# Seven block products in place of eight: key, query and feed-forward projections as Strassen units ahead of attention

## The chip, the cores and the metric

The kernel runs on one core of one Trainium2 chip. A core has five engines that run their own instruction streams and meet through semaphores: TensorE (PE; it multiplies matrices, and loads the stationary operand, called the weights, in a stream of its own, PEld), VectorE (DVE), ScalarE (ACT), GpSimd (POOL) and SyncE (SP, which here only starts transfers). PE writes its results into PSUM, eight banks of 128 x 512 floats; all other operands lie in SBUF. The metric is the time of one launch in microseconds (us).

## The reference

`x` is 2048 x 640. Two paths share it: a 32-head attention in four segments of 512 rows with a compressive memory, and a gated feed-forward block. A sigmoid gate mixes them.

```python
q, k, v = x @ wq, x @ wk, x @ wv            # 32 heads of 20
for s in range(4):                          # segments of 512 rows
    p = softmax(q[s] @ k[s].T * 20**-0.5 + mask)
    a_dot = p @ v[s]
    a_mem = phi(q[s]) @ M / (phi(q[s]) @ z + 1e-6)
    o[s] = g * a_mem + (1 - g) * a_dot
    M += phi(k[s]).T @ v[s];  z += phi(k[s]).sum()
a = o @ wo
b = (silu(x @ w1) * (x @ w3)) @ w2          # 640 -> 1728 -> 640
out = gate * a + (1 - gate) * b
```

Here `phi(t)` is `t + 1` for positive `t` and `exp(t)` otherwise. The results are wanted in float32 quality.

## The kernel before, in words

**Precision.** Each float32 matrix is split into a rounded high part and the rest (`split`, L115; `parts`, L290; `w_split`, L178). A product is three passes (`PASSES`, L261): high x high, high x low, low x high. With the contraction of 640 in five blocks of 128 (kb), one output block of 128 features x 512 rows is 15 matmuls of 512 columns (`proj`, L263).

**Chunks.** The 2048 rows are four chunks of 512 (c = 0 to 3), handled as two pairs, A = (0, 1) and B = (2, 3).

**Head.** Ahead of attention the program computes, for A: query blocks 0 and 1 (`q_blocks`), all values (`v_blocks`, L378), the five key blocks of each chunk (`k_block`, L423) and query block 2. Between the key blocks stand the memory steps: a transpose of phi(k) (`memory_turn`, L441: pkt) and its product with v (`memory_write`, L453: pm).

**Attention with filler.** Then 32 quads of four heads follow (`attention`, L810). Each quad has 40 slots. In a few slots stands a visit, a bundle of scores for the row maxima (s, L647), scores in transposed form (t, L682) and products with v (o, L703); `VISITS` (L807) says which bundle stands in which slot. A quad's s, t and o stand in three successive quads: the row maxima go from DVE (L654) by ACT, DVE and a transfer into two extra rows of `qk`, and only then t can run. Between the visits PE gets "dense" filler in portions: the rest of the projections, the feed-forward blocks (gate g and up u, `ffn_up`, L520; down f, `ffn_down`, L579) and the output projection (op). The jobs are listed in segments (`segs`), and each segment's work is spread evenly over the slots up to its end.

**Order and buffers.** PE's order is as the program is written. The other engines' order is set by a scheduler at build time, so they are in-order queues in a fixed order when they run. Weights go through six W buffers in rotation (NW, L27); POOL makes the two parts of each from W7 on (the cast L185, the subtraction L190). PSUM banks are given out in rotation (`bank_tile`, L121); a bank in which dense products accumulate is held until they are done.

Of the kernel before, what the change touches and what calls it, by code (L numbers as in the profile page):

```python
# [30 lines left out]
EARLY = range(2, 6)  # L31
OUT = {5: (0, 1), 6: (2, 3)}
# [6 lines left out]
def gated_mix(ctx: ExitStack, tc: tile.TileContext, xT, w01, wqk, wv, w13, w2, w2h, wo, beta, out):  # L39
# [81 lines left out]
    def bank_tile(name, hold=None):  # L121


        k = free.pop(0)
# [8 lines left out]
    def filled():  # L133

        free.extend(held)
        held.clear()
# [20 lines left out]
    items, tiles = [], {}  # L157

    def w_add(src, n, queue=nc.sync):
        items.append((src, n, queue))  # L160
        return len(items) - 1

    early, raws, clock = [], [], dict(step=0, oldest=2, next=2)

    def w_load():
        k = clock["next"]
        src, n, queue = items[k]
        if k in EARLY:
            if k % 2 == 0:
                early[:] = [sp.tile([P, 2, 1280], F32, tag="P32", name=f"wr{k}", bufs=NP)]  # L170
            raw = early[0][:, k % 2]
        else:
            raw = sp.tile([P, D + 2], F32, tag="wraw", name=f"wr{k}", bufs=NRAW)
        queue.dma_start(raw[:, :n], src)
        raws.append([k, raw, n, clock["step"]])
        clock["next"] += 1

    def w_split():  # L178
        k, raw, n, _ = raws.pop(0)
        w = sp.tile([P, 2, D + 2], FR, tag="W", name=f"W{k}", bufs=NW)  # L180
        tiles[k] = w
        if k < 7:
            split(w[:, :, :n], raw[:, :n], lo=nc.vector.tensor_sub)
        else:
            hi = nc.gpsimd.tensor_copy(w[:, 0, :n], raw[:, :n])  # L185
# [4 lines left out]
            last["low"] = nc.gpsimd.tensor_sub(w[:, 1, :n], raw[:, :n], w[:, 0, :n].bitcast(F32))  # L190

    def w_step():
# [3 lines left out]
        if raws and raws[0][0] in EARLY:  # L196
            if clock["step"] >= 6 + 2 * raws[0][0]:
                w_split()
        elif raws and raws[0][0] < clock["oldest"] + NW and \
                clock["step"] - raws[0][3] >= (AGE if "exp" in last or raws[0][0] < 7 else 2 * AGE + 1):  # L200
            w_split()
        if sum(r[0] not in EARLY for r in raws) < NRAW and clock["next"] < min(len(items), clock["oldest"] + NW + NRAW):
            w_load()

    def w_get(i, oldest=None):

        while i not in tiles:
            if not raws or raws[-1][0] < i and len(raws) < NRAW:
                w_load()
            else:  # L210
                w_split()
        clock["oldest"] = i if oldest is None else oldest
        return tiles[i]

# [225 lines left out]

    def memory_turn(c, mb):  # L441
# [76 lines left out]
    hts = {}  # L518

# [59 lines left out]
    def ffn_down(cs, js, idx, last=()):  # L579
        first = js[0] == 0  # L580
        w2s = [w_get(i, idx[0]) for i in idx]
        for c in cs:
# [135 lines left out]
    def o_sums(c):  # L718
# [4 lines left out]
        after(22 if c < NSEG - 1 else 3, o_scale, c, er)  # L723
# [85 lines left out]

    def attention():  # L810

        for m in range(-1, NQUAD + 2):
            for n in range(40):
# [3 lines left out]
                todo = VISITS.get(n, ()) if m != 1 else {BIG: VISITS[BIG][:3] + VISITS[BIG][4:5], BIG + 6: VISITS[BIG][5:]}.get(n, VISITS.get(n, ()))  # L817
# [10 lines left out]
                elif n in ((24, 36) if m < 0 else (BIG + (1 if m > 1 else 7), SMALL + 1)) and m + 1 < NQUAD:  # L828
# [43 lines left out]
    def job_up(cs, j):  # L872
        return (4 if j < NF else 2) * 3.5, ffn_up(cs, j, plan_up([j])[0])
# [72 lines left out]
    segs.append((2 * H - 2, seg))  # L946
# [23 lines left out]
    for n, (_, g) in enumerate(head):  # L970
# [3 lines left out]
        if n == 0:  # L974
            constants()
        elif n == 2:
            selection()
        elif n == 7:
            gates()
    stores(True)  # L980
    att = attention()
# [115 lines left out]
```

## Time and profile before

| what | value |
|---|---|
| runs of this kernel | 1099.22, 1099.38, 1100.0 us (median 1099.38) |
| profiled execution: its own time, from first to last instruction (span) | 1098.7 us |
| PE busy | 1093.1 us, 99% |
| PEld / DVE / ACT / POOL busy | 78% / 55% / 35% / 53% |
| HBM traffic over the span | 138 GB/s |

The page gives no other time for the profiled execution than its span; the median of the runs lies 0.7 us above it. The busy share is that of whole engines over all stages; matmuls are pipelined, so that the duration shown for one (some 0.4 us) is longer than the distance from one to the next. That distance is read from the chain of waits, where a run of matmuls stands with its count and its whole time.

### The profile page before, as it was taken

Reading aid. Unit: us, or ns where it says so; the run is one execution under the profiler, and the core shown is the slowest. Engines: PE = TensorE matmul, PEld = TensorE weight load, DVE = VectorE, ACT = ScalarE, POOL = GpSimd, SP = SyncE. Lnnn points to the kernel's source line nnn. Section 1 sums busy time; section 2 is a strip of 40 time slices with the busy share of each in tenths; the row PEclk is TensorE's granted clock in tenths of the full one; section 3 lists DMA queues with packets and bytes.
Section 4 is the critical chain, followed back from the end, with each engine's and each line's share of the span. In section 5 each row is a group of like instructions: output and inputs, shape, how many; then the busy total and the mean of one; then the engine's idle time right before and its main releaser. Section 6 shows DMA issues by size and latency. Waiting matters only on the chain.

```text
span 1098.7 us, 17910 instructions
## 1 busy us (share of the span) xinstructions
PE 1093.1 (99%) x6289; PEld 853.6 (78%) x6289; DVE 603.1 (55%) x1716; ACT 381.9 (35%) x829; POOL 584.2 (53%) x729
## 2 busy tenths in 40 slices
PE   9999999999999999999999999999999999999998
PEld 7988887777777777778977777777777777777787
DVE  6032474356555554566153678975657765551575
ACT  6244233443233122145244543424333332223020
POOL 5055556366366363566066447656674655565263
PEclk9999999999999999999999999999999999999999
DMA  9266943334355234435367966445664343432122
GB/s 314 105 207 222 284 123 82 95 83 117 77 141 124 58 85 124 137 83 184 112 201 264 298 216 185 112 148 140 161 149 111 96 113 97 111 102 89 52 79 96
DMA packets 87978, 153.21 MB, mean 139 GB/s; under 512 B 11632, under 2 KB 25872, under 8 KB 87888
## 3 DMA queue, kind: packets, MB, share of 16 engines
q1 hardware_dynamic: 63472, 106.30, 30.3%
q0 software_dynamic: 20384, 38.68, 15.6%
q10 hardware_dynamic: 4032, 7.08, 1.8%
q8 instruction: 50, 0.82, 0.3%
q14 instruction: 40, 0.33, 0.1%
HBM read 96.56 MB, written 54.54 MB: 138 GB/s over the span
## 4 chain that ended last, share of the span: by engine, by line
PE 99%; DMA 0%; ACT 0%; DVE 0%; SPq 0%; issue 0%
PE g L267 18%; PE f L593 18%; PE u L267 17%; PE o L703 7%; PE v L398 7%; PE op L852 6%; PE k L267 6%; PE q L267 5%; PE s L647 5%; PE t L682 4%; PE nd L365 2%; PE pm L462 1%; PE q L338 1%; PE gt L783 1%; PE pkt L447 1%; PE rr L777 0%
## 5 line engine op out<-in xcount | busy, mean ns | idle before, releaser
L654 DVE CUSTOM_DVE_ANT_0 junk<-s,mask 128x256 bf16<-128x256 f32 (+3 forms) x512 | 250.4, 489 | 106.1 <-PE s L647 74.0
L688 ACT ACTIVATE P<-t 128x512 f32<-128x512 f32 (+1 forms) x384 | 172.5, 536 | 187.7 <-PE t L682 145.1
L267 PE MATMUL g<-X,W 128*128 128x512 f32 x840 | 208.9, 398 | 0.1
L190 POOL TENSOR_TENSOR W<-wr,W 128x640 fp32r<-128x640 f32 (+1 forms) x126 | 198.8, 1583 | 2.5
L267 PE MATMUL u<-X,W 128*128 128x512 f32 x780 | 196.9, 399 | 0.0
L593 PE MATMUL f<-ht,W 128*128 128x512 f32 (+1 forms) x825 | 196.4, 395 | 0.0
L185 POOL CAST W<-wr 128x640 fp32r<-128x640 f32 (+1 forms) x126 | 92.6, 739 | 195.1 <-PE v L398 44.6
L693 POOL TENSOR_SCALAR_AFFINE_SELECT P<-P 128x256 f32<-128x256 f32 x192 | 93.6, 497 | 179.5 <-ACT P L688 179.2
L267 PEld LDWEIGHTS g<-X,W 128*128 128x128 f32 x840 | 155.8, 188 | 37.3 <-DVE m L654 0.4
L593 PEld LDWEIGHTS f<-ht,W 128*128 128x128 f32 x825 | 153.1, 188 | 36.3
L267 PEld LDWEIGHTS u<-X,W 128*128 128x128 f32 x780 | 144.0, 188 | 34.5 <-ACT P L688 0.3
L117 POOL TENSOR_TENSOR ht<-ft,ht 128x512 fp32r<-128x512 f32 x52 | 67.5, 1298 | 91.1 <-ACT ht L116 91.0
L624 POOL DMA_DIRECT2D qk<-qkd x128 | 83.3, 652 | 0.5 <-issue 0.2
L647 PE MATMUL s<-qk 60*128 60x256 f32 (+3 forms) x512 | 77.7, 346 | 0.0
L267 PE MATMUL k<-X,W 128*128 128x512 f32 x300 | 77.2, 404 | 0.0
L703 PE MATMUL o<-P,vg 128*32 128x512 f32 (+3 forms) x1024 | 75.5, 435 | 0.1
L533 ACT ACTIVATE ft<-g 128x512 f32<-128x512 f32 x52 | 31.2, 600 | 126.5 <-PE g L267 113.8
L534 DVE SCALAR_TENSOR_TENSOR fu<-ft,g 128x512 f32<-128x512 f32 x52 | 35.6, 685 | 67.9 <-ACT ft L533 58.8
L398 PE MATMUL v<-W,X 128*128 128x320 f32 (+1 forms) x480 | 72.1, 311 | 0.2 <-ACT P L688 0.2
L398 PEld LDWEIGHTS v<-W,X 128*128 128x128 f32 x480 | 71.2, 189 | 0.9 <-ACT P L688 0.4
L116 ACT CAST ht<-ft 128x512 fp32r<-128x512 f32 x52 | 32.2, 619 | 109.9 <-DVE ft L542 108.1
L601 DVE TENSOR_TENSOR acc<-f,acc 128x512 f32<-128x512 f32 x65 | 44.8, 689 | 39.5 <-PE f L593 39.2
(125 smaller groups left out, 1209.3 us busy)
## 6 DMA issues: line engine op xcount, KB each, us to landing
qk<-qkd POOLq DMA_DIRECT2D x128, 240.0 KB, 4.1
wr<-in_w_dram SPq DMA_DIRECT2D x80, 320.0 KB
qkd<-qs SPq DMA_DIRECT2D x20, 512.0 KB
qkd<-ks SPq DMA_DIRECT2D x20, 512.0 KB
od<-oq SPq DMA_DIRECT2D x32, 256.0 KB
wr<-in_wo_dram SPq DMA_DIRECT2D x20, 320.0 KB
vg<-vd SPq DMA_DIRECT2D x16, 336.0 KB
xr<-in_xT_dram SPq DMA_DIRECT2D x20, 256.0 KB
```

Of the source, the lines that this page charges most:

```text
L117: (lo or nc.gpsimd.tensor_sub)(dst[:, 1], src, dst[:, 0].bitcast(F32))
L185: hi = nc.gpsimd.tensor_copy(w[:, 0, :n], raw[:, :n])
L190: last["low"] = nc.gpsimd.tensor_sub(w[:, 1, :n], raw[:, :n], w[:, 0, :n].bitcast(F32))
L267: nc.tensor.matmul(ps, w[:, a, kb * P:(kb + 1) * P], x[:, b, kb, :], start=n == 0, stop=n == 14)
L398: nc.tensor.matmul(ps[:, :n1 - n0], x[:, a, kb, lb * P:(lb + 1) * P], wvt[kb][:, b, n0:n1], start=n == 0, stop=n == 14)
L593: nc.tensor.matmul(ps[:, :n1 - n0], w, h, start=n == 0, stop=n == len(ms) - 1)
L624: here(nc.gpsimd.dma_start(t[64 * i:64 * i + RH], qkd[c][RH * (h + i):RH * (h + i + 1)]))
L647: nc.tensor.matmul(ps[i][:, o:o + w], q[:, qb * P:(qb + 1) * P], key[:, :w], start=n == 0, stop=n == len(todo) - 1, skip_group_check=True)
L654: r = nc.vector.tensor_tensor_reduce(out=junk[:, :w], in0=ps[i][:, o:o + w], in1=mask[:, L - w:], scale=1.0, scalar=-3.0e38, op0=ALU.add, ...
L688: last["exp"] = nc.scalar.activation(pairs[2 * m + k]["P"][:, i, o:o + n], ps[i][:, b:b + n], AF.Exp, scale=SCALE)
L693: nc.gpsimd.affine_select(d, d, pattern=[[0, 2], [0, n], [1, P]], base=0, channel_multiplier=-1, compare_op=ALU.is_ge, fill=0.0)
L703: nc.tensor.matmul(ps[32 * i:32 * i + 32, kb * P:], heads[2 * p + i]["v"][:, kb], pairs[p + i // 2]["P"][:, i % 2, o:o + n], start=kb == 0 ...
```

## The change

Four pairs of key and query blocks (K0 K1, K2 K3, K4 Q2, Q3 Q4) and the gate/up pairs of four feature blocks (0, 1, 2 and 3) are computed for chunks 0 and 1 as "units" (`unit`). A unit treats its two weight blocks, the two chunks and the first four contraction blocks as 2 x 2 matrices of blocks and forms seven products in place of eight, with sums and differences of the operands; the fifth contraction block is computed as before. The sums of the four x blocks are made once (`build_sums`, braided with the values), from x loaded again; they lie in `qk` and two wide buffers. For each unit DVE makes five sums of weight blocks (`w_split`, kind "sum0"), POOL splits four weight operands (of 640, 640, 512 and 384 columns), and the results are put together by DVE and ACT in the buffers W, V and G.

All eight units stand ahead of attention, with the down product of feature blocks 0 to 2 between the third and the fourth feed-forward unit. Thus query blocks 3 and 4 and a part of the feed-forward work leave attention's filler, and the job lists of the first two segments are shorter. Further edits: `ffn_down` of the first two groups starts with three feature blocks side by side (`lead`: three held banks) and with chunk 1 or 3 first; the visits of the first two quads are spread by a table of their own (`FIRST`); constant rows of `qk` and `vg` are set by DVE behind the units; the loads of the first two head pairs are issued in the last unit.

```diff
-        for v in vg:
-            nc.gpsimd.memset(v[:, :, VG:], 0.0)
-        one = cp.tile([P, KB, L], F32, tag="oall", name="one", bufs=1)[:, 0]
-        nc.gpsimd.memset(one, -1.0)
-        for i in range(4):
-            nc.gpsimd.tensor_copy(qk[i // 2][:, 1, i % 2], one)
+    def fixed_rows():
+        for t in qk:
+            nc.vector.memset(t[:, 1].bitcast(F32), -1.0)
+        nc.vector.memset(vg[0][:, :, VG:], 0.0)
...
+        elif kind == "sum0":
+            low = raws[rs[1]][0]
+            sums[rs[1]] = t = f_tile(f"ws{k}")
+            a11, a12, a15 = raw[:, :2 * P], raw[:, 2 * P:4 * P], raw[:, 4 * P:D]
+            a21, a22, a25 = low[:, :2 * P], low[:, 2 * P:4 * P], low[:, 4 * P:D]
+            nc.vector.tensor_add(t[:, 2 * P:], a21, a22)
+            nc.vector.tensor_sub(t[:, :2 * P], a11, a21)
+            nc.vector.tensor_sub(a11, t[:, 2 * P:], a11)
+            nc.vector.tensor_sub(a12, a12, a11)
+            nc.vector.tensor_sub(a15, a15, a25)
...
+    def build_sums(cs):
+        c0, c1 = cs
+        raw, two = {}, []
+        def load(i):
+            for n, (c, kb) in enumerate(((c1, 2 + i), (c1, i), (c0, i), (c0, 2 + i))):
+                raw[i, n] = f_tile(f"tr{c0}_{i}_{n}")
+                nc.sync.dma_start(raw[i, n], xT[c, :, kb, :])
...
+            b22, b12, b11, b21 = (raw[i, n] for n in range(4))
+            nc.vector.tensor_sub(b22, b22, b12)
+            nc.vector.tensor_sub(b12, b12, b11)
+            nc.vector.tensor_add(b11, b22, b11)
+            split(out(2, i), b11, lo=nc.vector.tensor_sub)
+            yield 1
+            split(out(1, i), b12, lo=nc.vector.tensor_sub)
+            nc.vector.tensor_sub(b21, b21, b11)
+            yield 1
+            split(out(3, i), b22, lo=nc.vector.tensor_sub)
+            yield 1
+            split(out(4, i), b21, lo=nc.vector.tensor_sub)
...
+    def unit(cs, name, idx, take, W, V, G):
+        c0, c1 = cs
+        T = lambda n: lambda i, b: Ts[n, i][:, b]
+        B = lambda c, kb: lambda i, b: Xs[c][:, b, kb + i]
+        def product(ps, w, col, x, n, start=False, stop=False):
+            t = 0
+            for i in range(n):
+                for a, b in PASSES:
+                    nc.tensor.matmul(ps, w[:, a, col + i * P:col + (i + 1) * P], x(i, b),
+                                     start=start and t == 0, stop=stop and t == 3 * n - 1, skip_group_check=True)
+                    t += 1
+                if i < n - 1:
+                    yield 699
+        w0, wa, wb, wl = idx
+        U = w_get(w0, w0)
+        a, ka = bank_tile(f"{name[0]}{c0}_{name}", 1300), last["k"]
+        yield from product(a, U, 0, B(c0, 0), 2, True, True)
+        nc.scalar.copy(W, a)
+        yield 699
+        S0 = w_get(wa, w0)
+        w, kw = bank_tile(f"w{c0}_{name}", 1300), last["k"]
+        yield from product(w, S0, 0, T(2), 2, True, True)
+        filled(kw)
+        nc.vector.tensor_add(W, W, w)
+        yield 699
+        S1 = w_get(wb, w0)
+        x, kx = bank_tile(f"x{c1}_{name}", 1300), last["k"]
+        yield from product(x, S1, 2 * P, T(1), 2, True)
+        yield 699
+        A2 = w_get(wl, w0)
+        yield from product(x, A2, 2 * P, B(c1, 4), 1, False, True)
+        nc.scalar.copy(V, x)
+        yield 699
+        y, ky = bank_tile(f"y{c0}_{name}", 1300), last["k"]
+        yield from product(y, S1, 0, T(3), 2, True, True)
+        nc.vector.tensor_add(V, V, y)
+        nc.vector.tensor_add(V, V, W)
+        gone.add(wb)
+        if name[0] != "f":
+            take(1, c1, V)
+        yield 699
+        yield from product(a, U, 2 * P, B(c0, 2), 2)
+        yield 699
+        yield from product(a, U, 4 * P, B(c0, 4), 1, False, True)
+        filled(ka)
+        gone.add(w0)
+        take(0, c0, a)
+        yield 699
+        yield from product(x, S0, 2 * P, B(c1, 2), 2)
+        yield 699
+        yield from product(x, S0, 4 * P, B(c1, 4), 1, False, True)
+        filled(kx)
+        gone.add(wa)
+        g = G if G is not None else f_tile(f"ug{name}")
+        nc.vector.tensor_add(g, W, x)
+        take(0, c1, g)
+        if name[0] == "f":
+            take(1, c1, V)
+        yield 699
+        yield from product(y, A2, 0, T(4), 2)
+        yield 699
+        yield from product(y, A2, 2 * P, B(c0, 4), 1, False, True)
+        filled(ky)
+        nc.vector.tensor_add(W, W, y)
+        take(1, c0, W)
+        clock["oldest"] = wl + 1
...
+        def take(i, c, ps):
+            w, mb = blocks[i]
+            if w:
+                big["k", c, mb] = phi = pks.pop(0)
+                out.append((c, mb))
+            else:
+                phi = big["q", c][:, mb * L:(mb + 1) * L] if c else None
+            store_parts(w, c, mb, parts(f"{'qk'[w]}s{c}_{mb}", ps, phi))
...
+            if i == 0:
+                us[c] = u = f_tile(f"fu{c}_{j}")
+                nc.scalar.activation(u, ps, AF.Tanh, scale=0.5)
+                nc.vector.scalar_tensor_tensor(u, u, 1.0, ps, op0=ALU.add, op1=ALU.mult)
+            else:
+                nc.vector.scalar_tensor_tensor(us[c], us[c], 0.5, ps, op0=ALU.mult, op1=ALU.mult)
+                split(hts[c, j], us[c], lo=nc.vector.tensor_sub)
+            if i == 0 and c == cs[0] and j == sum(GROUPS[:2], [])[2 + NU]:
+                fixed_rows()
+                for p in range(2):
+                    load_pair(p)
...
+        lead = js in GROUPS[:2]
+        for c in cs[::-1] if lead else cs:
             if first:
                 accs[c] = slot(f"acc{c}")[:, :KB * L].rearrange("p (b n) -> p b n", b=KB)
-            for fb in range(KB):
+            if lead:
+                two = [bank_tile(f"f{c}_{js[0]}_{fb}_0", 1300) for fb in range(3)]
+                for n, j in enumerate(js):
+                    for fb, ps in enumerate(two):
+                        for i, (a, b) in enumerate(PASSES):
+                            nc.tensor.matmul(ps, w2s[n][:, b, fb * P:(fb + 1) * P], hts[c, j][:, a],
+                                             start=n == i == 0, stop=(n, i) == (len(js) - 1, 2))
+                        yield 699
+                filled()
+                for fb, ps in enumerate(two):
+                    dst = accs[c][:, fb]
+                    if first:
+                        nc.scalar.copy(dst, ps)
+                    else:
+                        nc.vector.tensor_add(dst, ps, dst)
+            for fb in range(3 if lead else 0, KB):
...
+    s, t = (lambda f: ("s", 0, f)), (lambda f: ("t", 1, f))
+    FIRST = ({5: (s(0),), 8: (s(2),), 11: (s(1),), 14: (s(3),), 17: (s(4),)},
+             {5: (s(0), t(0), t(1), t(3)), 11: (s(2), t(2), s(1)), SMALL: VISITS[SMALL]})
...
-    head = qa + job_v(A)
+    head = qa + [braid(chain(job_v(A)), (0, build_sums(A)), 3)]
     load_wide(1)
-    ka, turns, writes = jobs_k(A)
-    q2 = job_q(A, 2)
-    head += ka + q2[:1] + turns + q2[1:] + writes
+    K0, K1, K2, K3, K4 = ((1, mb) for mb in range(KB))
+    head += jobs_qk(A, ((K0, K1), (K2, K3), (K4, (0, 2)), ((0, 3), (0, 4))))
+    head += [job_unit(A, j) for j in GROUPS[0]] + [job_down(A, 0)]
+    head += [job_unit(A, j) for j in GROUPS[1][:NU]]
+    clock["wide"] = len(items)
     segs = []
-    seg = job_q2(A, 3)
-    g = jobs_group(A, 0)
-    seg += [braid(chain(g[:2]), job_read(1), 3, at=(7, 10, 13, 16, 18, 22, 25, 28))] + g[2:] + jobs_group(A, 1) + jobs_up(A, 2)
+    seg = [job_up(A, j) for j in GROUPS[1][NU:]] + [job_down(A, 1)]
+    g = jobs_group(A, 2)
+    seg += [braid(chain(g[:2]), job_read(1), 3, at=(9, 12, 15, 18, 21, 24, 27, 30))] + g[2:] + jobs_up(A, 3)
     segs.append((H + LAG + 1, seg))
-    d = job_down(A, 2)
-    u = [job_up(A, j) for j in GROUPS[3][:2]]
+    d = job_down(A, 3)
     o1, o2 = jobs_oproj(0)
-    seg = [d, braid(chain(u), o1, 5), o2] + [job_up(A, j) for j in GROUPS[3][2:]] + [(0, load_shares(A[:1])), job_down(A, 3)]
+    seg = [braid(d, o1, 3, at=(13, 15, 17, 19, 20)), (0, load_shares(A[:1])), o2]
```

**PE, the start of the key stage.** In the names k is a key block, then the chunk (`k0_...`); ge is a small transpose; in the changed kernel w, x, y are further products of the unit, W7 to W10 the four weight operands, T and qk the sums of x, X0 and X1 the chunks. Before:

```order
L267 MATMUL k0_0_618<-X0_103,W7_276 128x512 x9
L419 MATMUL ge0_628<-ident_88,gate_102 8x128
L267 MATMUL k0_0_618<-X0_103,W7_276 128x512 x6
L267 MATMUL k1_0_647<-X1_105,W7_276 128x512 x9
L419 MATMUL ge1_670<-ident_88,gate_102 8x128
L267 MATMUL k1_0_647<-X1_105,W7_276 128x512 x6
L447 MATMUL pkt0_0_688<-ident_88,pk0_0_639 128x128 x4
L267 MATMUL k0_1_695<-X0_103,W8_594 128x512 x12
L462 MATMUL pm0_0_711<-V0_302,pkn0_0_693 128x147 x4
```

Now:

```order
L544 MATMUL k0_k0k1_664<-X0_103,W7_268 128x512 x6
L544 MATMUL w0_k0k1_685<-qk1_91,W8_626 128x512 x6
L469 MATMUL ge0_694<-ident_88,gate_102 8x128
L544 MATMUL x1_k0k1_698<-qk0_90,W9_643 128x512 x6
L469 MATMUL ge1_705<-ident_88,gate_102 8x128
L544 MATMUL x1_k0k1_698<-X1_105,W10_651 128x512 x3
L544 MATMUL y0_k0k1_714<-T0_319,W9_643 128x512 x3
L544 MATMUL y0_k0k1_714<-T1_447,W9_643 128x512 x3
L544 MATMUL k0_k0k1_664<-X0_103,W7_268 128x512 x9
L544 MATMUL x1_k0k1_698<-X1_105,W8_626 128x512 x9
L544 MATMUL y0_k0k1_714<-T0_319,W10_651 128x512 x3
```

Key blocks 0 and 1 of both chunks were 60 matmuls on two weight operands; they are now 54 matmuls on four. The second operand, W8, is now wanted after 6 matmuls; before it was wanted after 30.

**POOL, the same place.** `CAST` makes a weight operand's high part, `TENSOR_TENSOR` its low part. Before:

```order
L99 AFFINE_SELECT sel_96<-sel_96 32x640
L102 COPY sel_96<-sel_96 32x640 x2
L185 CAST W8_594<-wr8_271 128x640
L185 CAST W9_605<-wr9_279 128x640
L190 TENSOR_TENSOR W8_594<-wr8_271,W8_594 128x640
L190 TENSOR_TENSOR W9_605<-wr9_279,W9_605 128x640
L174 DMA wr10_597<-in_wqk_dram 128x640
L174 DMA wr11_608<-in_wqk_dram 128x640
```

Now:

```order
L186 DMA wr8_263<-in_wqk_dram 128x640
L226 TENSOR_TENSOR W7_268<-wr7_181,W7_268 128x640
L221 CAST W8_626<-wr7_181 128x640
L221 CAST W9_643<-ws8_627 128x512
L221 CAST W10_651<-wr8_263 128x384
L221 CAST W11_668<-wrs_292 128x640
L226 TENSOR_TENSOR W8_626<-wr7_181,W8_626 128x640
L226 TENSOR_TENSOR W9_643<-ws8_627,W9_643 128x512
L226 TENSOR_TENSOR W10_651<-wr8_263,W10_651 128x384
```

Four casts now stand ahead of the subtraction that completes W8; before there were two.

**PE in the middle of attention, quad 26.** s, t are scores of the quad in the name, f is a down product. Before, from the end of the first visit of the quad to its second:

```order
L647 MATMUL s26_1_0_9150<-qk0_90 128x384
L647 MATMUL s26_1_1_9151<-qk0_90 128x384
L647 MATMUL s26_1_0_9150<-qk0_90 128x128
L647 MATMUL s26_1_1_9151<-qk0_90 128x128
L593 MATMUL f3_3_1_0_9167<-ht3_3_8444,W97_8454 128x512 x3
L593 MATMUL f3_3_1_0_9167<-ht3_4_8587,W98_8530 128x512 x3
L593 MATMUL f3_3_1_0_9167<-ht3_5_8823,W99_8691 128x512 x3
L593 MATMUL f3_3_2_0_9178<-ht3_3_8444,W97_8454 128x512 x3
L593 MATMUL f3_3_2_0_9178<-ht3_4_8587,W98_8530 128x512 x3
L593 MATMUL f3_3_2_0_9178<-ht3_5_8823,W99_8691 128x512 x3
L593 MATMUL f3_3_3_0_9189<-ht3_3_8444,W97_8454 128x512 x3
L593 MATMUL f3_3_3_0_9189<-ht3_4_8587,W98_8530 128x512 x3
```

Now:

```order
L892 MATMUL s26_1_0_9294<-qk0_90 128x384
L892 MATMUL s26_1_1_9295<-qk0_90 128x384
L892 MATMUL s26_1_0_9294<-qk0_90 128x128
L892 MATMUL s26_1_1_9295<-qk0_90 128x128
L892 MATMUL s26_3_0_9311<-qk0_90 128x256
L892 MATMUL s26_3_1_9312<-qk0_90 128x256
L892 MATMUL s26_3_0_9311<-qk0_90 128x256
L892 MATMUL s26_3_1_9312<-qk0_90 128x256
L927 MATMUL t25_4_0_9325<-qk1_91 128x384
L927 MATMUL t25_4_1_9326<-qk1_91 128x384
L927 MATMUL t25_4_0_9325<-qk1_91 128x128
L927 MATMUL t25_4_1_9326<-qk1_91 128x128
```

The 24 dense matmuls that stood between the two visits are gone from there; the second visit now follows the first at once.

## Rows read from the trace of the kernel before

**Rows 1.** Page, first line and section 1: PE's busy time

```profile
span 1098.7 us, 17910 instructions
...
PE 1093.1 (99%) x6289; PEld 853.6 (78%) x6289; DVE 603.1 (55%) x1716; ACT 381.9 (35%) x829; POOL 584.2 (53%) x729
```

**Rows 2.** Page, section 2: granted TensorE clock in 40 slices (9: full speed)

```profile
PEclk9999999999999999999999999999999999999999
```

**Rows 3.** Waits of PE: engine, line <- whom: us in total, times, longest

```profile
PE warm L921 <- DVE zero L918: 1.3, 1, 1.3
PE q L338 <- ACT w01s L116: 0.2, 1, 0.2
PE v L398 <- ACT P L688: 0.2, 1, 0.2
```

**Rows 4.** Chain of waits in order of time: start us, us, what

```profile
22.32 33.89 PE v L398 x227
...
68.83 2.83 PE k L267 x12
73.80 2.79 PE k L267 x12
...
353.15 20.99 PE f L593 x90
```

**Rows 5.** Stretches of the values and the keys: us, busy time and instructions by engine

```profile
25.00:50.00 25.00, 25.00 (x171) 25.00 (x170) 0.52 (x3) 5.55 (x18) 3.66 (x6) 1.00 0.35 128
75.00:100.00 25.00, 25.00 (x137) 21.43 (x136) 7.62 (x15) 12.17 (x28) 16.54 (x26) 1.00 0.68 228
```

**Rows 6.** Timeline from 50 to 62 us: start us, us, engine, line, what

```profile
54.56 1.38 POOL L185 CAST W<-wr 128x640 fp32r<-128x640 f32 x2 [25.71 <-PE v L398]
55.91 3.09 POOL L190 TENSOR_TENSOR W<-wr,W 128x640 fp32r<-128x640 f32 x2
...
56.06 2.27 PE L267 MATMUL k<-X,W 128*128 128x512 f32 x9
...
57.53 1.49 DVE L413 TENSOR_SCALAR gate<-gate 128x4 f32<-128x4 f32 x1
```

**Rows 7.** Page, section 5: groups of instructions, busy us, mean ns

```profile
L654 DVE CUSTOM_DVE_ANT_0 junk<-s,mask 128x256 bf16<-128x256 f32 (+3 forms) x512 | 250.4, 489 | 106.1 <-PE s L647 74.0
...
L190 POOL TENSOR_TENSOR W<-wr,W 128x640 fp32r<-128x640 f32 (+1 forms) x126 | 198.8, 1583 | 2.5
...
L601 DVE TENSOR_TENSOR acc<-f,acc 128x512 f32<-128x512 f32 x65 | 44.8, 689 | 39.5 <-PE f L593 39.2
```

**Rows 8.** Groups by form: a DVE subtraction with both inputs in SBUF

```profile
L786 DVE TENSOR_TENSOR oall<-on,gm 128x512 fp32r<-128x512 f32 x15 | 13.6, 915 | 2.1 <-ACT gm L785 2.1
```

**Rows 9.** Tile X on DVE: ns min/median/max

```profile
L117 DVE TENSOR_TENSOR X<-xr,X x7: 692/694/3148, 4.2 to 13.7; 128x512 fp32r<-128x512 f32 x7
```

**Rows 10.** Timeline from 385 to 392 us: one POOL and one DVE subtraction

```profile
387.69 1.29 POOL L117 TENSOR_TENSOR ht<-ft,ht 128x512 fp32r<-128x512 f32 x1 [0.88 <-ACT ht L116]
388.23 1.30 DVE L786 TENSOR_TENSOR oall<-on,oT 128x512 fp32r<-128x512 f32 x1 [0.69 <-ACT oT L785]
```

**Rows 11.** Chain of waits in order of time, 760 to 781 us

```profile
760.97 0.43 PE s L647 x2
...
765.48 3.67 PE f L593 x15
769.14 0.43 PE s L647 x4
...
770.10 2.98 PE f L593 x12
...
780.09 0.43 PE s L647 x2
```

More of the change, by code (lines that the diff above doesn't have):

```diff
@@ L131, in bank_tile, with filled @@
         return ps
[L133 to L136 removed]
+    def filled(*ks):
+        for k in ks or list(held):
+            del held[k]
+            free.append(k)
     def split_psum(dst, src, name, pin=lambda ins: ins):
@@ L155, in f_tile, with w_add_unit @@
         return sp.tile([P, L], F32, tag="f", name=name, bufs=4)
-    items, tiles = [], {}
+    items, prods, tiles = [], [], {}
     def w_add(src, n, queue=nc.sync):
         items.append((src, n, queue))
-        return len(items) - 1
-    early, raws, clock = [], [], dict(step=0, oldest=2, next=2)
+        prods.append(("all", (len(items) - 1,)))
+        return len(prods) - 1
+    def w_add_unit(src0, src1, queue=nc.sync):
+        items.extend((src, D, queue) for src in (src0, src1))
+        r = len(items) - 2
+        prods.extend((("all", (r,)), ("sum0", (r, r + 1)), ("sum1", (r + 1,)), ("low", (r + 1,))))
+        return list(range(len(prods) - 4, len(prods)))
+    early, raws, clock, gone = [], {}, dict(step=0, oldest=2, next=2, made=2), set()
+    spare, sums = [], {}
     def w_load():
@@ L171, in w_load @@
             raw = early[0][:, k % 2]
+        elif spare and k < clock["wide"]:
+            raw = spare.pop(0)
         else:
@@ L189, in w_split @@
                                   reason="weights in order")
-            last["low"] = nc.gpsimd.tensor_sub(w[:, 1, :n], raw[:, :n], w[:, 0, :n].bitcast(F32))
+            last["low"] = nc.gpsimd.tensor_sub(w[:, 1, :n], src, w[:, 0, :n].bitcast(F32))
+        if kind in ("sum0", "low") or kind == "all" and (k + 1 == len(prods) or prods[k + 1][0] != "sum0"):
+            w_free(rs[0])
     def w_step():
         clock["step"] += 1
-        if raws and raws[0][0] in EARLY:
-            if clock["step"] >= 6 + 2 * raws[0][0]:
+        k = clock["made"]
+        if k < len(prods) and all(r in raws for r in prods[k][1]):
+            live = sum(i >= clock["oldest"] and i not in gone for i in range(2, k))
+            if k in EARLY:
+                if clock["step"] >= 6 + 2 * k:
+                    w_split()
+            elif live < NW and clock["step"] - max(raws[r][2] for r in prods[k][1]) >= \
+                    (AGE if "exp" in last or k < 7 or prods[k][0] != "all" else 2 * AGE + 1):
                 w_split()
[L199 to L202, printed above, removed]
+        if clock["next"] < len(items) and (spare and clock["next"] < clock["wide"] or sum(
+                r not in EARLY and not any(raws[r][0] is x for x in wide) for r in raws) < NRAW):
             w_load()
@@ L207, in w_get, with wide_raws @@
         while i not in tiles:
-            if not raws or raws[-1][0] < i and len(raws) < NRAW:
+            if all(r in raws for r in prods[clock["made"]][1]):
+                w_split()
+            else:
                 w_load()
-            else:
-                w_split()
         clock["oldest"] = i if oldest is None else oldest
         return tiles[i]
+    wide = []
+    def wide_raws():
+        t = sp.tile([P, 2, 1280], F32, tag="P32", name="wrs", bufs=NP).rearrange("p a n -> p (a n)")
+        wide.extend(t[:, i * (D + 2):(i + 1) * (D + 2)] for i in range(3))
+        spare.extend(wide)
     Xs, accs, w01s = {}, {}, []
@@ new lines, in qk_unit, with turn, turned @@
+    def qk_unit(cs, blocks, idx, prev):
+        out = []
+        def take(i, c, ps):
[6 more added lines that the diff above has]
+            store_parts(w, c, mb, parts(f"{'qk'[w]}s{c}_{mb}", ps, phi))
+        def turn(c):
+            gate_turn(c)
+            yield 100
+        def turned(c, mb):
+            pks.append(big["k", c, mb])
+            yield from memory_turn(c, mb)
+        name = "".join("qk"[w] + str(mb) for w, mb in blocks)
+        steps = [turn(c) for c in cs]
+        if prev:
+            steps = [f(*d) for mb in sorted({mb for _, mb in prev}) for f in (turned, memory_write)
+                     for d in sorted(prev) if d[1] == mb]
+        n = 0
+        for y in unit(cs, name, idx, take, *rest[:3]):
+            yield y
+            n += 1
+            if n >= 4 and n % 2 == 0 and steps:
+                yield from steps.pop(0)
+        prev[:] = out
```

76 lines of the change are left out of this document (63 added, 13 removed).

## The prediction

> **What bounds the kernel now.** I read the page's first lines, then PE's waits, then the chain in order of time. PE is busy for 1093.1 of 1098.7 us [rows 1], and the granted clock is in its top tenth in every slice, the 2.4 GHz level [rows 2]. PE waits for other engines for 1.7 us in all, and 1.3 of them are the start [rows 3]. So the time is the sum of what PE streams, and a change is worth the matmuls that it takes from PE, less the waits that it puts in their place. The price of a matmul comes from the chain: 90 of 512 columns take 20.99 us, 0.233 us each [rows 4]; a piece of the keys agrees (12 in 2.83 us, 0.236). The other engines have room on average (DVE 55%, POOL 53%), but what counts is the stage in which the new work stands.
>
> **What is removed.** A unit replaces 4 x 15 = 60 matmuls. Its seven products of two contraction blocks are 7 x 2 x 3 = 42; the fifth block adds 4 x 3 = 12. That is 54, all of 512 columns, and the order of PE shows them (6, 6, 6, 3, 6, 9, 9, 9). Eight units save 48 matmuls, 48 x 0.233 = 11.2 us. All else on PE (memory steps, down products, scores) keeps its count. This is the only gain. The head grows: eight units and one down product of 90 matmuls stand there, but they are moved, not added.
>
> **The first unit's wait.** POOL can make the second operand W8 only when the values let go of a W buffer, at 54.56 us in this trace; PE starts the keys at 56.06 [rows 6]. Before, W8 was wanted 30 matmuls later, now after 6, and its low part by the third matmul of its product: 56.06 + 8 x 0.233 = 57.9. POOL now does four casts first: two of 640 columns took 1.38 us [rows 6], so 640 + 512 + 384 + 640 columns take 2.3 us, to 56.9; the casts wait for one buffer after another, so I take 57.1. The subtraction of W8 takes 1.58 [rows 7], to 58.7. PE waits 0.8 us. Bounds: 0, if the scheduler's order is luckier than I read it; 2.8 us, if DVE's operations get in between (a tiny gate operation took 1.49 there [rows 6]). I take 0.8. What follows (W9 at 60, W10 at 61) comes before PE asks.
>
> **DVE and POOL inside the units.** Between the units everything is prepared one unit ahead, so no wait follows from order alone; the question is throughput. A feed-forward unit lasts 54 x 0.233 = 12.6 us. DVE has 16 instructions in it: 11 of 512 columns and five sums of 256 or 128. At 0.69 [rows 7] and half of that for the narrow ones (an estimate) they take 7.6 + 1.7 = 9.3 us. Eleven of the sixteen have both inputs in SBUF. Such an operation takes 0.69 alone, too, but has a tail: the X subtractions have median 0.694 and maximum 3.15 us [rows 9], and the trace shows why: one started at 388.23, POOL's subtraction ran to 388.98, and the DVE one ended 0.55 us later, after 1.30 us [rows 10]. Operations that read PSUM have no such tail (0.689 in the mean [rows 7]). The mean of the kind is 0.915 [rows 8], 0.23 more. So a unit costs DVE 9.3 + 11 x 0.23 = 11.8 us of 12.6: it fits, with little to spare. POOL has 2176 columns to split: 2176/640 x 1.58 = 5.4 us of subtractions and 2.5 us of casts, 7.9 us; it fits. A key unit has 18 DVE instructions, 10.7 + 12 x 0.23 = 13.5 us; the first lasts 13.1 on PE with two small transposes, the later ones 12.6 plus two or four memory steps of 1.47 each (the distance of two pieces of the keys, 4.97, less 15 matmuls, 3.50) [rows 4]; that is 18.5 us with four. A small lag of the first is made up there.
>
> *Rule weighed:* the Trainium skill, SBUF — State Buffer, section Who interferes with whom, says that a DVE instruction with two SBUF inputs and a GpSimd instruction that reads SBUF exclude each other for a whole instruction. The trace agrees ([rows 10]: 1.30 in place of 0.69). By it the worst case is that none of POOL's 5.4 us passes beside such DVE work, which is the first rival below.
>
> Bounds for this term: 0 from below (a gain is excluded: PE does not get faster by another engine's work). From above: per unit all 5.4 us of subtractions add to DVE: 14.7 against 12.6 in four feed-forward units, 4 x 2.1 = 8.4, and 16.1 against 13.1 in the first key unit, 3.0; together 11.4 us. I take 1.2 us, near the bottom, because the mean operation [rows 8], not the longest, is the nearest row.
>
> **Covered at no cost.** The sums of x: 16 DVE and 8 ACT operations and eight loads of 256 KB lie beside the values, where DVE is busy 0.5 of 25 us, ACT 5.6, the transfers 0.35 [rows 5]; at 0.92 the DVE work is 15 us within some 36. If that cover failed, the second product of the first unit would be late. The stores on SP's queue wait for parts as before; the weight loads queued behind them are for units two ahead. The constants leave POOL's start, where nobody waited. The first pairs' loads wait for DVE's fixed rows, and these for products of the last unit; behind them on POOL stand only weights for filler, and 51 dense matmuls (11.9 us) stand between the unit's end and the first scores. ACT gets two copies per unit; beside the keys it was busy 12.2 of 25 us [rows 5].
>
> **Attention with less filler.** The moved work leaves the first 16 quads. In a quad with short filler the trace shows PE at the first visit from 760.97 to 765.48, at the second from 769.14 to 770.10, and at the next quad's first at 780.09: 5.5 us of visits, 13.6 of filler, 19.1 us in all, without a wait [rows 11]. Counted in the order, the first segment's quads come to about 20 us, the second's to 30. But by the order single quads are thinner: I count 54 and 45 dense matmuls ahead of the second and third o, and, because the three held banks of the down product push visits about, 39 in quad 22; in quad 26 both visits stand together. With 5.5 us of visits these are 18.1, 16.0 and 14.6 us. DVE needs 250.4/32 = 7.8 us for the maxima of one quad [rows 7] plus a copy and the way to the extra rows of qk. Nothing in the trace is shorter than the 19.1 of rows 11, so the upper bound is that each is stretched to it: 1.0 + 3.1 + 4.5 = 8.6 us; the lower is 0. I take 2.0, nearer to the bottom, since at 19.1 PE did not wait at all.
>
> **Sum.** Against the profiled execution: 1098.7 - 11.2 + 0.8 + 1.2 + 2.0 = 1091.5 us. The median of the runs is 0.7 above that execution, so I predict 1092.2.
>
> **Rivals.**
> 1. *DVE outlasts the units, slower.* Place: the first key unit and the four feed-forward units. DVE's two-input operations wait out POOL's subtractions in full, the next weights come late, PE waits in every unit. For it: [rows 9, 10] and the many such operations; POOL often has its four casts and subtractions back to back. Against: the median operation does not wait, and PSUM reads can pass. Price 11.4 in place of 1.2: 1099.4 - 11.2 + 0.8 + 11.4 + 2.0 = 1102.4. It decides once the two-input mean passes 0.69 + (12.6 - 9.3)/11 = 0.99 us; it was 0.915. Chance 0.10.
> 2. *The thin quads give the gain back.* The path from maxima to t doesn't fit into less than 19.1 us: 8.6 in place of 2.0, 1099.4 - 11.2 + 0.8 + 1.2 + 8.6 = 1098.8. For it: such quads never occurred. Against: DVE's 7.8 us leave room. Chance 0.09. A mixture of half of both rivals gives about the same.
> 3. *Every wait is hidden.* 1099.4 - 11.2 = 1088.2. For it: all lower bounds are 0. Against: the arithmetic of the first unit. Chance 0.12.
> 4. *It doesn't do what it says*, that is, a unit's matmuls are slower for their mixed operands, so that 54 take as long as 60. For it: nothing in the rows, which hold no such operands. Against: the order shows the same columns and one load per matmul as before. 1099.4; chance 0.02.
>
> **How the numbers follow.** The forecast, 1089 to 1096 us, holds 0.67. A measurement of this kernel tells 0.2%, about 2 us, from no change. Faster by more (below 1097.2): forecast and rival 3, 0.79. Within it: rivals 2 and 4, 0.11. Slower (above 1101.6): rival 1, 0.10. For 8 in 10 I go from 1088 to 1099.5, which leaves out rival 1 and a part of 2.
>
> **What would show it.** Right: PE with 48 fewer matmuls; one wait of about 1 us of PE for POOL's W at the start of the keys; DVE near 90% busy in the feed-forward units and PE full; PE's waits in all a few us. Wrong by rival 1: long PE waits for W in units two to eight, two-input DVE operations above 1 us in the mean. Wrong by rival 2: PE waiting for `qk` or for banks of s in quads 2, 22 and 26. The forecast falls, too, if the granted clock drops behind a wait of PE, which no slice shows now.

## The result and the profile after

The changed kernel takes 1103.0 us (median of 8 runs, 1099.9 to 1104.0), the one before 1099.9 (8 runs, 1099.2 to 1100.1): ratio 1.0023, 95% interval 1.0014 to 1.0032. I had said 1092.2 (1088 to 1099.5). It is slower by 3.1 us, about 11 from the forecast. Of its eight runs the five with a mean granted clock of 0.997 or 0.998 took 1102.9 to 1104.0, the three with 0.999 or 1.000 1099.9 to 1101.7.

The page, first line and section 1, and the shares of the chain by engine in section 4, after the change:

```profile
span 1101.1 us, 18012 instructions
...
PE 1088.2 (99%) x6241; PEld 847.0 (77%) x6241; DVE 680.8 (62%) x1824; ACT 394.4 (36%) x853; POOL 610.9 (55%) x747
...
PE 95%; POOL 2%; DVE 1%; ACT 1%; issue 0%; DMA 0%; ACTq 0%; DVEq 0%; POOLq 0%
```

Beside [rows 1], PE has exactly 48 matmuls fewer, and yet the span is 2.4 us longer. A full PE row hides this: the chain is PE for only 95%. Waits of PE (engine, line, releaser: us in total, times, longest), beside [rows 3]; in names like x_k2k the first letter is the unit's product, the rest its blocks:

```profile
PE s L892 <- DVE m L899: 1.7, 3, 0.6
PE t L927 <- DMA qk<-mr: 1.5, 1, 1.5
PE g L317 <- DVE m L899: 1.4, 2, 0.7
...
PE x_k2k L544 <- POOL W L226: 1.0, 1, 1.0
PE w_k0k L544 <- POOL W L226: 0.4, 1, 0.4
```

The last two are the units, the first three attention; the start (1.3, as before) and waits of 0.3 and less are left out. This view understates them, because a wait that runs under the modelled end of a matmul isn't counted. The chain in order of time (start us, us, what) says more. First the units, where rival 1 expects the loss (a feed-forward unit's last two products and the down product behind them):

```profile
155.74 2.07 PE x_ff L544 x9
157.81 2.10 PE y_ff L544 x9
159.91 6.31 PE f L820 x27
```

Here matmuls of units take 0.232 us each, one product on another without a gap. Now quad 22, the same stretch of attention as [rows 11]:

```profile
762.16 2.29 PE o L948 x32
...
765.76 1.59 PE f L838 x6
767.35 0.48 PE s L892 x4
...
767.88 0.56 DVE junk L899
...
772.66 0.29 DVE junk L899
...
774.51 0.52 ACTq L915
...
775.07 3.79 DMA qk<-mr
...
779.00 0.73 PE t L927 x6
779.73 2.29 PE o L948 x32
```

From the scores that end at 767.83 to the first t of the next visit (779.00) the path is maxima on DVE (`junk`), 5 us; the negated maxima and their transposes, 1.6; the issue, 0.5; and a transfer of 3.79: 11.2 us that no filler can shorten. Only 33 dense matmuls (7.7 us) stand there now. And quad 26, where both visits stand together, by stretches of 10 us (busy PE, PEld, DVE, ACT, POOL with their instructions, granted clock, DMA share, GB/s):

```profile
840.00:850.00 10.00, 10.00 (x47) 7.84 (x47) 3.54 (x6) 0.00 (x0) 0.00 (x0) 1.00 0.05 10
850.00:860.00 10.00, 9.74 (x71) 6.20 (x68) 7.32 (x26) 5.34 (x12) 6.04 (x11) 0.83 0.37 82
```

ACT and POOL have nothing to do for 10 us, then all has to be done at once. The chain goes by DVE's maxima here, for which the scores wait:

```profile
853.26 0.68 DVE junk L899
...
855.89 0.50 PE s L892 x2
```

Behind this wait the granted clock falls from 1.00 to a mean of 0.83 (between its levels of 2.4 and 1.2 GHz), back at 1.00 from 860. In the 40 slices of the page nothing of this shows, the row reads as [rows 2].

### The profile page after: what moved, and what is told of

Read it like the earlier page. It is cut to its first block, busy times and chain, and to the rows that moved or that the text cites. A ratio compares the mean times of both kernels' runs of the same rounds, so it can differ in the third digit from the quotient of the medians.

```text
span 1101.1 us, 18012 instructions
## 1 busy us (share of the span) xinstructions
PE 1088.2 (99%) x6241; PEld 847.0 (77%) x6241; DVE 680.8 (62%) x1824; ACT 394.4 (36%) x853; POOL 610.9 (55%) x747
## 4 chain that ended last, share of the span: by engine, by line
PE 95%; POOL 2%; DVE 1%; ACT 1%; issue 0%; DMA 0%; ACTq 0%; DVEq 0%; POOLq 0%
PE g L317 15%; PE u L317 14%; PE f L838 13%; PE op L1101 6%; PE o L948 6%; PE v L448 6%; PE s L892 5%; PE f L820 4%; PE t L927 4%; PE q L317 3%; PE k L317 3%; PE nd L415 2%; PE x_ff L544 2%; PE pm L693 1%; PE q L388 1%; PE y_ff L544 1%
## 5 line engine op out<-in xcount | busy, mean ns | idle before, releaser
L226 POOL TENSOR_TENSOR W<-wr,W 128x640 fp32r<-128x640 f32 (+2 forms) x118 | 186.3, 1584 | 2.2
L317 PE MATMUL g<-X,W 128*128 128x512 f32 x720 | 179.8, 399 | 1.6 <-DVE m L899 1.4
L221 POOL CAST W<-wr 128x640 fp32r<-128x640 f32 (+2 forms) x118 | 87.8, 749 | 149.0 <-PE v L448 32.1
L317 PE MATMUL u<-X,W 128*128 128x512 f32 x660 | 166.9, 399 | 0.0
L317 PEld LDWEIGHTS g<-X,W 128*128 128x128 f32 x720 | 133.2, 188 | 33.8 <-DVE m L899 2.2
L838 PE MATMUL f<-ht,W 128*128 128x512 f32 (+1 forms) x609 | 148.9, 399 | 0.3 <-ACT P L933 0.3
L838 PEld LDWEIGHTS f<-ht,W 128*128 128x128 f32 x609 | 114.0, 190 | 27.2 <-ACT P L933 0.5
L892 PEld LDWEIGHTS s<-qk 60*128 60x128 f32 x512 | 46.8, 185 | 26.9 <-issue 18.8
L927 PE MATMUL t<-qk 62*128 62x256 f32 (+3 forms) x512 | 62.5, 321 | 2.0 <-DMA qk<-mr 1.5
L948 PEld LDWEIGHTS o<-P,vg 128*32 128x32 f32 x1024 | 30.2, 110 | 41.4 <-issue 31.9
```

Of the source, the lines that this page charges most:

```text
L221: hi = nc.gpsimd.tensor_copy(w[:, 0, :n], src)
L226: last["low"] = nc.gpsimd.tensor_sub(w[:, 1, :n], src, w[:, 0, :n].bitcast(F32))
L317: nc.tensor.matmul(ps, w[:, a, kb * P:(kb + 1) * P], x[:, b, kb, :], start=n == 0, stop=n == 14)
L838: nc.tensor.matmul(ps[:, :n1 - n0], w, h, start=n == 0, stop=n == len(ms) - 1)
L892: nc.tensor.matmul(ps[i][:, o:o + w], q[:, qb * P:(qb + 1) * P], key[:, :w], start=n == 0, stop=n == len(todo) - 1, skip_group_check=True)
L927: nc.tensor.matmul(ps[i][:, o:o + L - kb * P], key[:, kb * P:(kb + 1) * P], q[:, kb * P:], start=n == 0, stop=n == len(todo) - 1, skip_gro ...
```

## The experiments

The theory after the result: the saving is real and survives the units; it is given back where the down product with three banks at once (`lead` in `ffn_down`) meets attention. Rival: DVE and POOL beside the units. A dense matmul that an interval has less is counted at 0.232 us. Each time is a median; the kernel before had 1099.5 to 1099.7 beside these runs.

**e1, the interleaved down product for chunks A only** (`lead` also sets which chunk comes first, so for B the order of the chunks goes back, too).

```diff
-        lead = js in GROUPS[:2]
+        lead = js in GROUPS[:2] and cs[0] == 0
```

> The changed kernel, but with the first three banks of a down product interleaved for chunks A alone; for chunks B the down products of groups 0 and 1 go bank by bank as before the change. Theory (the gain is given back in attention, half of it where B's interleaved down product moves the visits of quads 22 and 26): the 3.7 and 3.0 us of extra wait in those two quads go, 1103.0 - 6.7 = 1096.3 us, and the granted clock no longer falls behind quad 26. Rival (the loss is in the units, where DVE and POOL are over 80% busy): nothing changes, 1103.

1096.9 us, 0.9977 of before [0.9967, 0.9986]. The chain at the same place, now with 57 dense matmuls between the two o, the products with v (39 in the changed kernel, and 63 for 81 ahead of the first):

```profile
757.45 2.29 PE o L948 x32
...
761.05 3.71 PE f L838 x15
...
765.72 2.97 PE f L838 x12
768.69 3.52 PE g L317 x15
772.21 3.47 PE u L317 x15
...
776.58 2.29 PE o L948 x32
```

The rows left out are PE's, too. From o to o it is 19.13 us, after the change 17.57 with 18 matmuls (4.2 us) less: 2.6 us of wait. The interval ahead of it loses 1.0 by the same count (26.41 with 81, 21.26 with 63). The interval of quad 26, 850.26 to 873.66 with 59 dense, is 26.11 here with 83: 2.9 us. Together 6.5; the spans differ by 6.1, the medians too. Of these, the fall of the clock is a part (e5). The stretch with the clock reads 1.00 here:

```profile
850.00:860.00 10.00, 10.00 (x53) 7.73 (x53) 6.17 (x25) 2.07 (x5) 6.66 (x8) 1.00 0.37 81
```

**e2, interleaved in the head only.**

```diff
-        lead = js in GROUPS[:2]
+        lead = js == GROUPS[0] and cs[0] == 0
```

> As e1, and A's group 1, whose down product stands at the start of attention, also goes bank by bank: the interleaved form is left in the head alone. Theory: the stall of 223 to 233 us in quad 1 (three banks held through its visits) goes too, about 2 us more than e1, 1094.3 us, below the kernel before. Rival (quad 1 stalls because its maxima follow each other too closely, whatever banks are held): as e1, 1096.3.

1093.9 us, 0.9946 [0.9934, 0.9959]: 3.0 below e1. In the changed kernel quad 1 goes so (chain in order of time):

```profile
223.72 0.73 POOL W L221
...
225.57 1.97 ACT P L933 x4
...
228.16 0.69 DVE junk L899
...
232.40 0.49 PE s L892 x2
```

and in e2:

```profile
224.85 0.61 ACT P L933
...
225.59 1.63 PE f L838 x6
...
229.38 0.54 DVE junk L899
...
231.73 0.50 PE s L892 x2
```

With three banks held for the down product the chain goes for nearly 9 us by P (the exponentials that ACT makes of t) and maxima, which give banks back to the scores; with one held, 0.6 and 2.4 remain. PE works beside most of this; what it loses is the 3.0. Whether the banks or the place of the visits did it here wasn't taken apart: e2 changes both (72 dense matmuls for 54 ahead of the next o).

**e3, that one edit in the kernel before** (its `ffn_down` gets the interleaved form, with `lead = js in GROUPS[:2] and cs[0]`).

> The kernel before the change, with that one edit of it: chunks B's down products of groups 0 and 1 interleave their first three banks. No Strassen, head and early quads as before. Theory: the same two quads have the same 81 and 39, 93 and 59 dense matmuls, so the same 6.7 us are lost, 1099.9 + 6.7 = 1106.6 us. Rival (the interleaving only hurts together with the change's other edits): 1099.9.

1104.4 us, 1.0046 [1.0033, 1.0058]. The edit alone (interleaving and order of the chunks together) costs 4.7 us without any Strassen product. It is 1.4 less than B's part in the changed kernel (6.1), and 2 less than expected; the fall of the clock is 1.3 (e5). In the profile the o-to-o intervals lose 3.0 up to the end of quad 22 and 1.7 in quad 26, and the granted clock doesn't fall there.

**e4, ordinary blocks in place of the units' products.** `unit` becomes, for both weights and both chunks,

```diff
+                for kb in range(KB):
+                    for a, b in PASSES:
+                        nc.tensor.matmul(ps, w[:, a, kb * P:(kb + 1) * P], Xs[c][:, b, kb],
+                                         start=n == 0, stop=n == 14)
```

and the sums of x and of the weights go.

> The changed kernel with every unit as its four ordinary blocks of 15 matmuls, in the same place: 48 matmuls more in the head (831 instead of 783 dense ahead of the second quad's product), no sums of blocks on DVE, no second load of x; attention is instruction for instruction the same on TensorE. Theory: Strassen's saving is real and all of it arrives, 48 x 0.232 = 11.1 less the 0.9 us of waits that its head has over the one before, so 1103.0 + 10.2 = 1113.2 us. Rival (sums on DVE and POOL take the saving back inside the units): 1103 to 1106.

1110.0 us, 1.0094 [1.0080, 1.0108]: 7.0 above the changed kernel, between the two. Part of the difference is the clock: the changed kernel's fell in the profiled run behind quad 26, this one's not, though TensorE's instructions in attention are the same: 1.3 us by the interval (23.40 us there, 22.07 here). So the products were priced again without stalls:

**e6, the same with e2's edit.**

> e4 (four ordinary blocks in place of each unit) with e2's edit, so that nothing of attention stalls: the price of Strassen's products alone, free of clock drops. Theory: 48 x 0.232 = 11.1 less up to 1.5 us of waits in the units, 1093.9 + 9.6 to 11.1 = 1103.5 to 1105.0 us; the move by itself (without Strassen) then costs 4 to 5 us against the kernel before. Rival (e4's 7.0 us is all that the products give): 1100.9.

1102.6 us, 1.0030 [1.0018, 1.0041]. Against e2 the 48 matmuls are worth 8.6 us of 11.2, less than the 9.6 to 11.1 I expected; 2.6 stay in the units and behind them. Two gaps, one at the first unit and one at K2K3's third product (e9), make up 1.3 of it by the waits of PE and 1.8 by the distances of the matmuls' starts; 0.5 lies behind the last matmul, where e2 ends 0.5 us later than e6, for a reason not found. Moving the blocks ahead of attention without Strassen, together with the change's other edits, so costs 3.1 us. Some 2 of that show in the intervals up to the tenth to thirteenth o, where filler became thinner (89 to 115 dense matmuls in place of 135 to 171); what causes them stays open.

**e5, place of the visits or banks held?** e2, but the visits wait as if the three banks were held, while the down product goes bank by bank:

```diff
+                delay[:] = [1] if late and fb < 3 else []
...
-                    if not held:
+                    if not held and not delay:
                         break
+                elif delay:
+                    pass
```

> e2 (the interleaved down product in the head alone), but the visits of attention that meet B's down products of groups 0 and 1 are put where the changed kernel has them: behind the third bank (81 and 39, 93 and 59 dense matmuls ahead of the products of quads 20 to 25), with the down product itself still bank by bank and one bank held at a time. Theory a (the place of the visits is what costs): the 3.7 us of quad 22 and 1.5 to 2.9 us of quad 26 come back on e2's 1093.9, 1099.1 to 1100.5 us. Theory b (three banks held at once starve the visits of banks): 1093.9.

1099.7 us, 1.0003 [0.9994, 1.0012], 5.8 above e2: theory b is out, but theory a's number is met in part by luck. With one bank held, quad 22 (17.34 us with 39 dense matmuls, 19.13 with 57 in e2) loses 2.4 and quad 26 1.6 (in the changed kernel, without its fall of the clock, 2.6 and 1.6). The other 1.6 lie ahead of quad 26, where the bank-by-bank product waits for its own operand `ht`, and the changed kernel loses nothing; ahead of quad 22, where that loses 1.0, e5 loses nothing: a visit there stands behind 33 dense matmuls, in the changed kernel behind 12. The chain shows the path of quad 22 again:

```profile
763.91 0.48 PE s L896 x4
...
771.64 3.56 DMA qk<-mr
...
775.33 0.74 PE t L931 x6
```

Its clock stays at 1.00 from 850 to 860, and the interval of quad 26 is 22.12 us (848.27 to 870.39) with the same 59 matmuls, 1.3 less than in the changed kernel: that is what the fall of the clock costs; the bunching costs 1.6. No run has the order of B's chunks turned round by itself, so that the place of the visits, and not this order, loses the time is read from the chains alone.

**e7 and e8, one and two units more.** If only the place matters, less filler should not.

```diff
-NU = 1
+NU = 2
```

(3 in e8.)

> e2 with one feature block more (five instead of four) as a unit ahead of attention: 12 matmuls fewer, 2.8 us, and quads 1 to 8 thinner (60, 45, 60, 63, 72, 60, 60 dense matmuls instead of 72, 45, 75, 60, 75, 60, 75; the last maxima of a quad to its first t 36 to 39 dense matmuls in five quads). Theory (PE waits only where the visits are bunched, 40 dense matmuls between s and t are enough, as in the kernel before in quads 18 to 22): 1093.9 - 2.8 = 1091.1 us. Rival (thin filler as such costs): 1093 or more.

> e2 with two feature blocks more (all of group 1) as units ahead of attention: 24 matmuls fewer, 5.6 us, quads 1 to 8 at 45, 45, 57, 54, 69, 45, 60 dense matmuls. Theory: with 35 to 51 dense matmuls between s and t still nearly no wait, 1 us at most, 1088.3 to 1089.3 us. Rival (thin filler as such costs): 1093 or more.

1096.7 us, 0.9974 [0.9964, 0.9984], and 1104.0, 1.0041 [1.0027, 1.0054]. Both missed by far: 2.8 and 10.1 us above e2, where 2.8 and 5 below it were expected. But little of it lies in the thin quads. From the third o on the intervals of e8 with 57, 54, 69 and 60 dense matmuls have no more than e2's; one with 45 loses 2.1. The losses stand ahead of the first two o. In e7 (chain):

```profile
231.50 1.56 POOL W L226
233.06 0.62 POOL qk L869
233.68 6.00 DMA qk<-qkd
...
239.82 0.39 PE s L892
```

The load of the next heads' rows is issued by POOL late, behind casts and subtractions of weights, and lands 6.0 us later; behind PE's wait the granted clock falls (0.82 in the mean from 242 to 250 us). In e8 the bank-by-bank down product follows the last unit at once, whose last operand stands on DVE behind two fills of `qk`:

```profile
212.81 0.91 DVE qk L77
...
214.43 0.91 DVE qk L77
...
222.01 3.00 DVE ht L117 x2
...
225.06 10.12 PE f L838 x34
```

PE waits here, and the clock falls behind the wait: 0.88 in the mean from 215 to 225 us, 0.69 from 225 to 232.

**e10, e7 with that load asked for earlier.**

```diff
-elif n in (() if m < 0 else (BIG + (1 if m > 1 else 7), SMALL + 1)) and m + 1 < NQUAD:
+elif n in (() if m < 0 else (6, 13) if m == 0 else (BIG + (1 if m > 1 else 7), SMALL + 1)) and m + 1 < NQUAD:
```

> e7 (five feature blocks as units) with the loads of head pairs 2 and 3 asked for at slots 6 and 13 of quad 0 instead of 12 and 18. Theory (what e7 lost is the 6.0 us transfer into qk that POOL issues late, at 233.1 us, behind its casts, and the clock that fell behind this wait; the thinner quads behind it cost nothing): 2.8 us below e2, up to 1 us of quad 1's maxima given back, 1091.1 to 1092.1 us. Rival (thin filler as such): 1096.7 as e7.

1093.2 us, 0.9940 [0.9927, 0.9952]: 3.5 of e7's loss came from this one transfer and what followed it. It stays 1.1 above the range expected, with one wait of 1.3 us of the first t for `qk<-mr`. It is the fastest of all, 6.4 us below the kernel before.

**e9, the selection matrix later** (`elif n == 2:` ahead of `selection()` becomes `n == 8`).

> e2 with the selection matrix (POOL's five instructions on sel, some 4.5 us of POOL) built five units later. Theory (the one wait of PE inside the units, 1.3 us ahead of K2K3's third product at 72 us, stands behind these on POOL): it shrinks to the 0.2 us of any other product, 1093.9 - 1.1 = 1092.8 us. Rival (the weights of that product are late by their own sums and splits): 1093.9.

1094.0 us, 0.9951 [0.9939, 0.9964]: nothing gained. The waits of PE from 40 to 205 us:

```profile
PE f L820 <- ACT ht L116: 0.4, 1, 0.4
PE w_k0k L544 <- POOL W L226: 0.4, 1, 0.4
PE f L820 <- DVE ht L117: 0.3, 1, 0.3
```

The wait for K2K3's weights is gone, so the theory of its cause holds, and another has come in the down product behind the third feature block, whose `ht` is late. POOL runs the five instructions from 155 to 164 us now, and DVE operations there with both inputs in SBUF are longer than in e2 (`ws` 2.49 us for 1.79, `fu` 1.20 for 0.68).

**e11 and e12, e10 with the later matrix, and a longer lead.** (`LEAD` 30 for 20 in e12.)

> e10 with e9's later selection matrix. Theory: the two gains add, 1090.0 to 1091.0 us.

> e11 with 30 instead of 20 slots ahead of quad 0, so that the first maxima meet 54 instead of 39 dense matmuls behind the last unit and quads 1 to 7 have 45, 60, 54, 63, 63, 60, 60. Theory (only the start of attention is short of room): 0.5 to 1 us below e11, 1089.5 to 1090.5 us. Rival (the later start thins quads 1 to 7 below what their maxima need): above e11.

1094.4, 0.9953 [0.9941, 0.9966], and 1094.6, 0.9954 [0.9941, 0.9968]: both above e10. With the later matrix PE's wait of 1.0 at K2K3's third product goes, and 1.6 come in the down product: the last unit ends at 207.1 us in e12's profile, at 206.3 in e10's. In e11's it ends at 208.9; there the granted clock fell behind the new wait (0.83 in the mean from 160 to 170), in a run 1.2 us above the median. The longer lead gives nothing.

## Why the prediction was wrong

*The saving: right in count, 8.6 us in effect.* 48 matmuls of 0.233 went, as the order said. Without stalls (e2 against e6) they are worth 8.6; the 2.6 between is a little more than the 2.0 that I gave the units.

*The first unit's wait, 0.8, and DVE and POOL, 1.2: right in size.* PE's gap at the first unit is 0.6 us by the matmuls' starts; the other is one of 1.2 at K2K3's third product, where I had none: I counted widths and left out the five instructions on `sel` that stand in POOL's queue there (e9). In the feed-forward units PE waits for nothing. DVE is busy 8.85 of 10 us from 150 to 160, POOL 9.07, where I had 11.8 of 12.6 and 7.9:

```profile
150.00:160.00 10.00, 10.00 (x45) 8.10 (x44) 8.85 (x10) 2.44 (x4) 9.07 (x7) 1.00 0.27 72
```

Operations on SBUF alone are longer there than those that read PSUM, as in [rows 8, 9] (groups of DVE by form, 125 to 193 us: busy us, mean ns):

```profile
L117 DVE TENSOR_TENSOR ht<-fu,ht 128x512 fp32r<-128x512 f32 x6 | 5.3, 904 | 0.2
...
L573 DVE TENSOR_TENSOR unit<-unit 128x512 f32<-128x512 f32 x4 | 4.3, 1068 | 0.1
...
L572 DVE TENSOR_TENSOR unit<-unit,y_ff 128x512 f32<-128x512 f32 x4 | 2.7, 686 | 1.5 <-PE y_ff L544 1.5
```

The Trainium skill, SBUF — State Buffer, section Who interferes with whom, gives a reason: a DVE instruction with two SBUF inputs contends with a GpSimd instruction that reads SBUF, and one waits until the other is done. The trace agrees, 0.90 to 1.07 against 0.69 us. Rival 1, the worst case of this, didn't come: over the 20 such operations of 512 columns of the feed-forward units in that stretch the mean is 0.98 us, just under the 0.99 at which I had said that it decides (in the key units `ks` took 1.31), and PE waits for none of them.

*"Attention with less filler", 2.0 with an upper bound of 8.6: this is the step that failed.* The places were right in part: quads 22 and 26 lost 3.6 and 2.9 us (e1, the first with the interval ahead of it). The price was not. I took a quad's whole length, 19.1 us in [rows 11], as what it needs, and gave each short quad the difference. What decides is not the length of a quad but how its filler is divided: from the last scores to the next t the path takes 11.2 us, and in quad 22 33 matmuls stood over it; in quad 26 both visits' maxima stand in a row with no matmul between. A quad with 54 or 57 matmuls, well divided, loses nothing (e8), and of the quads that I called thin at the second and third o, the third, with 45, shows no wait of PE (262 to 292 us). I had written down why the visits are displaced, and still took a value near the bottom because a quad of 19.1 us had not waited: that row speaks for its own division of filler, not for this one.

*Quad 1 was missing.* I priced it with the short quads (1.0 at most for its 54), but it holds the three banks through its visits: 2.7 us by the spans of e1 and e2, 3.0 by their medians; 1.8 of it lie ahead of the first o, where I had nothing. *So was the move itself*, 3.1 us by e6: my term was for single thin quads, and no run shows the cause.

*The clock* was named as what would make the forecast fall, with no price. It falls behind quad 26's wait, 1.3 us by the profile, in a part of the runs.

The account, by spans: forecast 1091.5; B's interleaved down product 6.1 (1101.1 less 1095.0), A's in attention 2.7 (1095.0 less 1092.3); the rest, 1092.3 for 1091.5, is the forecast's own 4.0 us of losses, measured at 4.8. That this rest came out within 0.8 is luck in part, as it holds the move, which I had not priced. Rival 2 named the path that failed, from maxima to t, for a reason that was wrong, the length of the quad, and had 0.09. Its 8.6 stand against 6.1 + 3.0 + 3.1 = 12.2 us lost outside the units by the medians (e1, e2, e6), of which no run puts the last 3.1 down to it. Of the slower cases I had only DVE; the one that came lay past rival 2's bound, which was no bound.

## What to carry to other kernels

Filler between latency-bound steps is worth nothing by its sum: list, for each step, the path that has to be covered (here 11.2 us from the last scores to the next t) and the matmuls that stand over just that path, before and after. An edit that only reorders the filler (banks interleaved, visits that wait for a bank to be done) can cost more than an algorithm saves, so try each edit of a bundle alone: one line, taken back, turned 1103.0 us into 1093.9. The work that a move puts in a stage's queues goes on to the next wait there (e9); look at what is late next, first of all at the point where the new stage hands over to the old one (e7, e8, e10).

## What the runs showed of the hardware

In the profiled executions the granted clock fell only behind waits of PE, and not every time: quad 26 stands behind a mean of 0.83 from 850 to 860 us in the changed kernel and 1.00 in e5 and e4, with the same order of matmuls there. The runs of the changed kernel spread over 4 us, those of e2, without that wait, from 1093.8 to 1094.1. So a part of the 3.1 us by which the changed kernel is slower comes and goes with the clock; how much beyond the 1.3 of the profile, no trace shows. Single runs of e1, e6, e9, e11 and e12 whose mean clock was 0.998 over the whole run were 1.2 to 2.4 us above the median of their kernel.

DVE work with both inputs in SBUF was longer beside POOL, 0.98 us in the mean for 0.69. The transfer of the maxima took 3.79 us (changed kernel, quad 22) and 3.56 (e5), as long as some 16 dense matmuls.
